# Weight splits, one softmax sum and the block means of v moved between engines in a fused attention and feed-forward kernel

## Chip, cores and metric

The kernel runs on one core of one Trainium2 chip. The metric is the device time of one execution in microseconds; a profile of one execution gives the times of single instructions. TensorE, VectorE, ScalarE and GpSimd are the engines that compute, SyncE (SP) issues the transfers. In the rows they are PE (PEld its weight loads), DVE, ACT, POOL and SP; a q behind a name is the engine's queue.

## The reference

```
k_sum = k in blocks of 32 tokens, max over the block     # 24 rows per head
v_sum = v in blocks of 32 tokens, mean over the block
scores = q k^T / 8, kept where |i - j| < 16; q k_sum^T / 8 + log 32
a = softmax over both kinds of scores together
x = a [v; v_sum]                       # 2 batches, 8 heads, 768 tokens, 64 wide
x = relu(x w_in)^2 w_out               # 1536 tokens, 512 -> 2048 -> 512
xn = x / rms(x) * rms_g
out = (silu(xn w_gate) * (xn w_val)) w_out2    # 512 -> 1536 -> 512
```

Inputs and output are float32, the weights float64 in memory: each is read as pairs of 32-bit words.

## The kernel before, in words

**Weights.** A unit is a weight tile of 128 x 512 (wi, wo of the first feed-forward; wg, wv, wp of the second), in the order of the list `order`. The class `Units` takes each through four steps: load the raw words (`load64`, L157), two ScalarE instructions (`conv_a`, L176 and L177), four VectorE instructions that put a float32 together (`conv_b`, L183 to L190), and `split` (L193): ScalarE casts to the format of the fast products (hi, L196), VectorE subtracts to get the rest (lo, L197). Every product is done as hi hi + hi lo + lo hi. Raw words, split weights and the raw q, k and v chunks share 14 buffers of tag "w".

**Attention** works on 12 groups of 128 tokens, 6 per batch. For a group g: `scores` (L417, TensorE), `softmax` (VectorE adds the mask L440 and takes the maximum; then either ScalarE does eight exponentials with the maximum as bias and sums by itself, L446, or VectorE subtracts L451, ScalarE does one exponential L452 and VectorE sums L453; `EXPACT(g)` says which; VectorE normalises, L454 to L456), `ptrans` (transposes L466, copy L467), `av` (products with the v rows in vx, L487, then split into xhi on ScalarE, L477, and xlo on VectorE, L478). Groups 0 to 2 do the softmax in two halves. `vload(g)` loads the group's v rows into vx, which holds two groups. Once per batch, the keys are loaded (`prep_load`), transposed (L327), reduced to block maxima (L330) and laid out with the maxima in gaps (L339, L340, `prep_kend` L344); the v means come from `vmean`: v is loaded in three chunks (`vm_load`) into "w" buffers, six products with an indicator matrix (L375) add rows of a block, and the result is copied to vm and from there to vx (L383, L384, `vmput` L390).

**Order.** Batch 1's first groups stand alone (L597 to L636). Then a loop over k_ from 0 to 5 (L695) interleaves a pair of groups each with the products of the first four wi (`h_pair`) and wo (`y_pair`) on the 256 tokens that are ready. Batch 2's keys are loaded at k_ 0, prepared within `y_pair(0, 2)`, its means formed at k_ 1 in front of group 7. After the loop come the other units of the first feed-forward (L759) and the second one (L790), on 512 tokens at a time.

The code is traced in this order, and a planner (L852) then orders each engine's instructions with its own cost model and puts in the waits: an instruction that it thinks ready can be placed ahead of earlier ones that wait. `issue_after` adds an edge on one engine's order. On the chip each engine's order is fixed, and the transfers of SP are one queue.

Of the kernel before, what the change touches and what calls it, by code (L numbers as in the profile page):

```python
# [32 lines left out]
def tile_window_attention_moe_moe2(  # L33
# [13 lines left out]
    nc = tc.nc  # L47
# [42 lines left out]
    um = cpool.tile([P, KW + QT], F32, name="um")  # L90
    masks = {}
    ind = cpool.tile([P, NB + P // (BLK // 2) * (NC2 - 1)], F32, name="ind")
    ss = cpool.tile([P, NG], F32, name="ss")
    rinv = cpool.tile([P, NG], F32, name="rinv")

    def constants():
        n = ind.shape[1]
        o = P // (BLK // 2) * (NC2 - 1)
        pb = BLK // 2
        nc.gpsimd.memset(ind, 1.0 / BLK)  # L100
        nc.gpsimd.affine_select(
            out=ind, in_=ind, compare_op=ALU.is_ge, fill=0.0, base=pb * o,
            pattern=[[-pb, n]], channel_multiplier=1,
        )
        nc.gpsimd.affine_select(
            out=ind, in_=ind, compare_op=ALU.is_ge, fill=0.0, base=pb - 1 - pb * o,
            pattern=[[pb, n]], channel_multiplier=-1,
        )
        nc.gpsimd.memset(um, 0.0)
        nc.gpsimd.affine_select(  # L110
            out=um, in_=um, compare_op=ALU.is_ge, fill=NEG, base=-1,
            pattern=[[1, KW + QT]], channel_multiplier=-1,
        )
        nc.gpsimd.affine_select(
            out=um, in_=um, compare_op=ALU.is_ge, fill=NEG, base=2 * WIN - 1,
            pattern=[[-1, KW + QT]], channel_multiplier=1,
        )


        mid = cpool.tile([P, NK], F32, name="mask_mid")  # L120
        nc.gpsimd.memset(mid, math.log(BLK))
        for j, n, o in ((0, G0, 0), (K1, QT, G0)):
            nc.gpsimd.tensor_copy(mid[0:QT, j : j + n], um[0:QT, o : o + n])
            nc.gpsimd.tensor_copy(mid[QT:P, j : j + n], um[QT:P, QT + o : QT + o + n])
        first = cpool.tile([P, NK], F32, name="mask_first")
        nc.gpsimd.tensor_copy(first, mid)
        nc.gpsimd.memset(first[0:QT, 0:WIN], NEG)
        last = cpool.tile([P, NK], F32, name="mask_last")
        nc.gpsimd.tensor_copy(last, mid)
        nc.gpsimd.memset(last[QT:P, NK - WIN : NK], NEG)  # L130
        masks.update(first=first, mid=mid, last=last)
# [58 lines left out]
        nc.vector.tensor_tensor(xi, xi, r, op=ALU.add)  # L190
        return x

    def split(x, nm):  # L193
        w_ = wslot(f"w_{nm}")
        hi, lo = w_[:, 0], w_[:, 1]
        nc.scalar.copy(hi, x)  # L196
        nc.vector.tensor_tensor(lo, x, hi.bitcast(F32), op=ALU.subtract)  # L197
        return hi, lo

    class Units:  # L200
# [9 lines left out]
        def tick(self):  # L210
            n, units = self.n, self.units
            if n[3] < n[2]:
                u = units[n[3]]
                W[u] = split(self.x.pop(u), "%s%d" % u)
                n[3] += 1
            if n[2] < n[1]:
                u = units[n[2]]
                self.x[u] = conv_b(*self.a.pop(u))
                n[2] += 1
            if n[1] < n[0]:  # L220
                u = units[n[1]]
                self.a[u] = conv_a(self.raw.pop(u), "%s%d" % u)
                n[1] += 1
            self.load(min(n[2] + self.ahead, len(units), self.used + self.cap))
# [9 lines left out]
                self.tick()  # L234

    def EXPACT(g):
        return g % 4 != 1

    def PARTS(g):
        return 2 if g < 3 else 1  # L240
# [101 lines left out]
    def prep_kend(b, eng, w0, w1):  # L342
# [3 lines left out]
            state[b].unsqueeze(2).to_broadcast([P, NPAIR, w1 - w0, NB]),  # L346
        )

    def vm_load(b, c):
        state[("v", b, c)] = raw_chunk(v, b, c, f"vr{b}_{c}")  # L350

# [14 lines left out]
    def vmean(b, c):  # L366

        if c == 0:
            state["vmps"] = psA(f"vmean{b}", [K1, DM])
        ps = state["vmps"][G0:K1]  # L370
        pb = BLK // 2
        nb2 = P // pb
        vr = state.pop(("v", b, c))
        for e in range(2):
            nc.tensor.matmul(  # L375
                ps, ind[:, nb2 * (NC2 - 1 - c) : nb2 * (NC2 - 1 - c) + NB], vr[:, :, e, :],
                start=(c == 0 and e == 0), stop=(c == NC2 - 1 and e == 1),
            )
        if c == NC2 - 1:
            vm = ap_.tile([K1, DM], F32, tag="vm", name=f"vm{b}", bufs=1)[G0:K1]  # L380
            state["vm"] = vm
            if b == 0:
                nc.vector.tensor_copy(vrows(0, 2), ps.unsqueeze(1).to_broadcast([NB, 2, DM]))  # L383
            nc.scalar.copy(vm, ps)  # L384

    def vrows(i0, n):
# [38 lines left out]
    def softmax(g):  # L425
        r = g % GPB
        mk = masks["first" if r == 0 else ("last" if r == GPB - 1 else "mid")]
        sl = state.pop(("s", g))
        te = ap_.tile([P, 2, NPAIR, NK], F32, tag="t", name=f"t{g}", bufs=TB)
        t = te.rearrange("q e p n -> q (e p) n")  # L430
        state[("t", g)] = t
        mx = ap_.tile([P, H], F32, tag="mx", name=f"mx{g}", bufs=TB)
        sm = ap_.tile([P, H], F32, tag="sm", name=f"sm{g}", bufs=TB)
        parts = PARTS(g)
        n = H // parts
        for i in range(parts):
            hs = slice(n * i, n * i + n)
            tv, m_, s_ = t[:, hs], mx[:, hs], sm[:, hs]
            for e in range(2 // parts * i, 2 // parts * (i + 1)):
                nc.vector.tensor_tensor(  # L440
                    te[:, e], sl[e], mk.unsqueeze(1).to_broadcast([P, NPAIR, NK]), op=ALU.add
                )
            if EXPACT(g):
                nc.vector.reduce_max(m_, tv, axis=AX.X, negate=True)  # L444
                for h in range(hs.start, hs.stop):
                    mark[("exp", g)] = nc.scalar.activation(  # L446
                        t[:, h], t[:, h], AF.Exp, bias=mx[:, h : h + 1], accum_out=sm[:, h : h + 1]
                    )
            else:
                nc.vector.reduce_max(m_, tv, axis=AX.X)  # L450
                nc.vector.tensor_tensor(tv, tv, m_.unsqueeze(2).to_broadcast([P, n, NK]), op=ALU.subtract)  # L451
                mark[("exp", g)] = nc.scalar.activation(tv, tv, AF.Exp)  # L452
                nc.vector.reduce_sum(s_, tv, axis=AX.X)  # L453
            nc.vector.tensor_scalar_add(s_, s_, 1e-9)  # L454
            nc.vector.reciprocal(s_, s_)
            mark[("norm", g)] = nc.vector.tensor_tensor(  # L456
                tv, tv, s_.unsqueeze(2).to_broadcast([P, n, NK]), op=ALU.mult
            )
# [235 lines left out]

    for k_ in range(NK2):  # L695
        g, last = 2 * k_ + 3, 2 * k_ + 3 >= NG
        if k_ == 0:
            for c in range(NC2):
                prep_load(1, c)
        h_pair(k_, 0)  # L700
        if k_ == 0:
            av(2)
            group(4)
        if not last:
            ptrans(g)
        if g == GPB - 1:
            group(GPB)
        h_pair(k_, 2)
        if not last:
            av(g)  # L710
        if g == GPB - 1:
            for c in range(NC2):
                vmean(1, c)
            vmput(0, 2)
        if g + 2 < NG:
            group(g + 2)
            if g + 2 == GPB + 1:
                vmput(2, 2)
        y_pair(k_, 0)
        if g + 1 < NG:  # L720
            ptrans(g + 1)
        if k_ == 0:
            prep_begin(1)
            prep_k(1, 0)
            y_pair(k_, 2, (lambda: prep_k(1, 1), lambda: prep_k(1, 2)))
            prep_kend(1, nc.gpsimd, 0, NW1)
            for c in range(NC2):
                vm_load(1, c)
        else:
            if g + 3 < NG:  # L730
                qprep(g + 3)
            y_pair(k_, 2)
        if g + 1 < NG:
            av(g + 1)
        if k_ == 0:
            qprep(GPB)
        elif g + 3 < NG:
            group(g + 3)
        if k_ == 2:
            units1.cap = NW - 3  # L740
        for _ in range(TICKS[k_]):
            units1.tick()
        if not last and g == NG - 1:
            actx.close()
            rot["tags"] = ("a",)
            side["pool"] = ctx.enter_context(
                tc.tile_pool(name="w2pool", bufs=1, side="right", reuse_waits="tile")
            )
            side["psum"] = ctx.enter_context(
                tc.tile_pool(name="psY2", bufs=1, space=PSUM, reuse_waits="tile")  # L750
            )
            grow = side["pool"].tile([P, DM], F32, tag="grow", name="grow")
            nc.sync.dma_start(grow, rms_g.partition_broadcast(P))
            units1.cap = NW + NRIGHT - 3
# [102 lines left out]
```

## Time and profile before

| | us |
|---|---|
| median of 3 runs | 668.42 (667.29 to 668.84) |
| the profiled execution | 668.78 |
| its span, first to last instruction | 667.1 |
| mean granted clock of TensorE | 0.982 of full speed |

The span is what the rows below lie in, in microseconds from its start; the 1.7 us around it belong to the execution. Busy time of an engine is summed over its instructions; records of TensorE are pipelined, so a full busy share there is not full speed by itself. Idle time counts only on the engine that the others wait for.

### The profile page before, as it was taken

How to read it: one execution, taken by the hardware profiler on the slowest of the kernel's cores; microseconds unless marked ns; L12 is line 12 of the kernel's file. 1: busy time of each engine (PE TensorE's matmuls, PEld its weight loads, DVE VectorE, ACT ScalarE, POOL GpSimd, SP SyncE). 2: the span in 40 equal slices, each digit the busy share in tenths (PEclk: the TensorE clock that was granted, in tenths of full speed). 3: DMA queues.
4: the chain of work that ended last, by engine and by line, in shares of the span. 5: the costliest groups of instructions: out<-in, count | busy, mean ns of one | idle time of the engine just before them, and what ended most of it. 6: DMA issues, size and time to landing. Idle time of an engine off the chain costs nothing.

```text
span 667.1 us, 9349 instructions
## 1 busy us (share of the span) xinstructions
PE 647.4 (97%) x3644; PEld 535.2 (80%) x3644; DVE 402.6 (60%) x729; ACT 306.5 (46%) x649; POOL 10.2 (2%) x29
## 2 busy tenths in 40 slices
PE   7789989999999999999999999999999999999997
PEld 6378857888888888888888888888888888888885
DVE  3999667759999279627574894289613171313132
ACT  4687667557775257226353873167411231111110
POOL 3000010000000000000000000000000000000000
PEclk8969999999999999999999999999999999999999
DMA  9993554315414123101120252015300000001011
GB/s 235 280 233 91 135 160 151 81 38 190 131 52 139 59 63 96 31 1 64 31 96 31 89 165 63 1 48 160 108 1 1 0 1 0 1 1 63 1 63 64
DMA packets 76956, 53.69 MB, mean 80 GB/s; under 512 B 45040, under 2 KB 71664, under 8 KB 76912
## 3 DMA queue, kind: packets, MB, share of 16 engines
q1 hardware_dynamic: 76912, 53.09, 26.9%
q8 instruction: 29, 0.48, 0.3%
q14 instruction: 15, 0.12, 0.1%
HBM read 49.94 MB, written 3.15 MB: 80 GB/s over the span
## 4 chain that ended last, share of the span: by engine, by line
PE 90%; DVE 4%; ACT 2%; DMA 1%; SPq 1%; issue 1%; DVEq 0%; ACTq 0%
PE y L529 19%; PE h L508 19%; PE v L508 15%; PE g L508 15%; PE z L529 14%; PE s L417 2%; PE vmean L375 2%; PE xps L487 2%; PE pps L466 1%; ACT t L446 1%; SPq L304 1%; DMA qr<-in_q_dram 1%; PE xps L499 1%; DVE mx L444 1%; DVE t L440 1%
## 5 line engine op out<-in xcount | busy, mean ns | idle before, releaser
L508 PE MATMUL h<-xhi,w_wi 128*128 128x512 f32 (+1 forms) x480 | 133.9, 352 | 0.0
L529 PE MATMUL y<-w_wo,hhi 128*128 128x512 f32 x384 | 118.0, 392 | 0.6 <-ACT hhi L519 0.6
L803 DVE TENSOR_TENSOR sg<-v,sg 128x512 f32<-128x512 f32 x36 | 24.9, 691 | 131.1 <-PE v L508 131.1
L508 PEld LDWEIGHTS h<-xhi,w_wi 128*128 128x128 f32 x480 | 86.2, 192 | 12.1 <-issue 0.3
L508 PE MATMUL v<-xhi,w_wv 128*128 128x512 f32 x288 | 94.7, 390 | 0.0
L508 PE MATMUL g<-xhi,w_wg 128*128 128x512 f32 x288 | 94.5, 390 | 0.0
L529 PE MATMUL z<-w_wp,hhiz 128*128 128x512 f32 x288 | 88.1, 389 | 0.0
L508 PE MATMUL h<-xlo,w_wi 128*128 128x512 f32 (+1 forms) x240 | 84.2, 352 | 2.8 <-DVE xlo L478 2.8
L529 PEld LDWEIGHTS y<-w_wo,hhi 128*128 128x128 f32 x384 | 71.2, 188 | 15.1 <-ACT hhi L519 0.9
L529 PE MATMUL y<-w_wo,hlo 128*128 128x512 f32 x192 | 73.4, 392 | 0.0
L801 ACT ACTIVATE sg<-g 128x512 f32<-128x512 f32 x36 | 21.5, 598 | 101.9 <-PE g L508 99.7
L508 PEld LDWEIGHTS v<-xhi,w_wv 128*128 128x128 f32 x288 | 54.1, 188 | 11.2
L529 PEld LDWEIGHTS z<-w_wp,hhiz 128*128 128x128 f32 x288 | 54.0, 188 | 11.2
L508 PEld LDWEIGHTS g<-xhi,w_wg 128*128 128x128 f32 x288 | 54.0, 188 | 11.1
L656 ACT ACTIVATE r<-h 128x512 f32<-128x512 f32 x48 | 28.7, 598 | 69.8 <-PE h L508 69.8
L508 PE MATMUL v<-xlo,w_wv 128*128 128x512 f32 x144 | 56.1, 389 | 0.0
L508 PE MATMUL g<-xlo,w_wg 128*128 128x512 f32 x144 | 56.0, 389 | 0.0
L529 PE MATMUL z<-w_wp,hloz 128*128 128x512 f32 x144 | 55.4, 389 | 0.0
L519 ACT CAST hhiz<-sg 128x512 fp32r<-128x512 f32 x36 | 22.3, 621 | 68.4 <-DVE sg L803 68.1
L657 DVE TENSOR_TENSOR r<-h,r 128x512 f32<-128x512 f32 x48 | 33.0, 687 | 34.1 <-ACT r L656 34.0
L508 PEld LDWEIGHTS h<-xlo,w_wi 128*128 128x128 f32 x240 | 46.1, 192 | 8.8 <-DVE xlo L478 3.0
L529 PEld LDWEIGHTS y<-w_wo,hlo 128*128 128x128 f32 x192 | 35.7, 188 | 7.3 <-issue 0.2
(129 smaller groups left out, 913.6 us busy)
## 6 DMA issues: line engine op xcount, KB each, us to landing
raw_wi<-in_moe_w_in_dram SPq DMA_DIRECT2D x16, 512.0 KB, 5.3
raw_wo<-in_moe_w_out_dram SPq DMA_DIRECT2D x16, 512.0 KB, 5.1
raw_wg<-in_moe_w_gate_dram SPq DMA_DIRECT2D x12, 512.0 KB, 3.6
raw_wv<-in_moe_w_val_dram SPq DMA_DIRECT2D x12, 512.0 KB, 3.5
raw_wp<-in_moe_w_out_dram SPq DMA_DIRECT2D x12, 512.0 KB, 3.5
kr<-in_k_dram SPq DMA_DIRECT2D x12, 256.0 KB, 4.2
qr<-in_q_dram SPq DMA_DIRECT2D x12, 256.0 KB, 4.1
vr<-in_v_dram SPq DMA_DIRECT2D x6, 512.0 KB, 5.9
```

What stands on the lines that cost most here:

```text
L304: nc.sync.dma_start(t[:, j].rearrange("p (h d) -> p h d", h=H), src[b, :, o : o + P, :].rearrange("h p d -> p h d"),)
L375: nc.tensor.matmul(ps, ind[:, nb2 * (NC2 - 1 - c) : nb2 * (NC2 - 1 - c) + NB], vr[:, :, e, :], start=(c == 0 and e == 0), stop=(c == NC2 - ...
L417: mark[("s", g)] = nc.tensor.matmul(sl[e][QT * u : QT * u + QT, p, :], qT[rr, p, QT * u : QT * u + QT], kT[rr, p, o : o + NK], start=True, ...
L440: nc.vector.tensor_tensor(te[:, e], sl[e], mk.unsqueeze(1).to_broadcast([P, NPAIR, NK]), op=ALU.add)
L487: nc.tensor.matmul(ps[QT * e : QT * e + QT, o : o + QT], vx[:, (2 * g + u) % NVX, 2 * p + e, :], pT[:, e * NPAIR + p, QT * u : QT * u + QT ...
L508: nc.tensor.matmul(ps, a_, b_, start=(i == 0), stop=(i == tot - 1))
L519: nc.scalar.copy(hi[:, 0:n], s[:, 0:n])
L529: nc.tensor.matmul(y, a_[:, ms], b_, start=(first and i == 0), stop=(last and i == 2))
L656: nc.scalar.activation(t, ps, AF.Relu)
L657: nc.vector.tensor_tensor(t, ps, t, op=ALU.mult)
L801: nc.scalar.activation(t, psg, AF.Silu)
L803: nc.vector.tensor_tensor(t, psv, t, op=ALU.mult)
```

## The change

- The first eight units (four wi, four wo) are split on GpSimd, copy and subtraction. The last GpSimd subtraction is kept as the mark "split".
- The first unit's `conv_b` is ordered on VectorE behind the last maximum of group 0.
- Group 1's softmax takes the ScalarE form (eight exponentials with sums).
- Batch 1's copy of the means into vx goes from VectorE (L383) to ScalarE.
- Batch 2's keys are loaded after group 5 instead of at the head of the loop.
- Batch 2's v is loaded by two transfers after group 4 into two x buffers (tags xhi and xlo), as 96 partitions of 8 tokens each, four heads to a buffer. GpSimd adds the 8 tokens in three steps (4, 2, 1 left) for each buffer, ordered behind "split"; two products of 256 columns with a new indicator over 96 partitions give the means, in place of six of 512 columns.

```diff
+    NE = 8
+    PV = S // NE
+    indv = cpool.tile([PV, NB], F32, name="indv")
...
+        pv = BLK // NE
+        nc.gpsimd.memset(indv, 1.0 / BLK)
+        nc.gpsimd.affine_select(out=indv, in_=indv, compare_op=ALU.is_ge, fill=0.0, base=0,
+            pattern=[[-pv, NB]], channel_multiplier=1)
+        nc.gpsimd.affine_select(out=indv, in_=indv, compare_op=ALU.is_ge, fill=0.0, base=pv - 1,
+            pattern=[[pv, NB]], channel_multiplier=-1)
...
-    def split(x, nm):
+    def split(x, nm, pool):
         w_ = wslot(f"w_{nm}")
         hi, lo = w_[:, 0], w_[:, 1]
-        nc.scalar.copy(hi, x)
-        nc.vector.tensor_tensor(lo, x, hi.bitcast(F32), op=ALU.subtract)
+        if pool:
+            nc.gpsimd.tensor_copy(hi, x)
+        else:
+            nc.scalar.copy(hi, x)
+        low = (nc.gpsimd if pool else nc.vector).tensor_tensor(lo, x, hi.bitcast(F32), op=ALU.subtract)
+        if pool:
+            mark["split"] = low
         return hi, lo
...
-                W[u] = split(self.x.pop(u), "%s%d" % u)
+                W[u] = split(self.x.pop(u), "%s%d" % u, n[3] < 2 * ROUNDS1[0])
...
-                self.x[u] = conv_b(*self.a.pop(u))
+                with after(*((("mx", 0),) if n[2] == 0 else ())):
+                    self.x[u] = conv_b(*self.a.pop(u))
...
     def EXPACT(g):
-        return g % 4 != 1
+        return g % 4 != 1 or g == 1
...
+    HH = H // 2
+    vsum = [xpool.tile([P, KD, CH], F32R, tag=t, name=f"vsum{t}") for t in ("xhi", "xlo")]
+    vsum = [
+        t.bitcast(F32).rearrange("p k s -> p (k s)").rearrange("p (h e d) -> p h e d", h=HH, e=NE)[0:PV]
+        for t in vsum
+    ]
+
+    def vs_load(b):
+        for i, t in enumerate(vsum):
+            nc.sync.dma_start(
+                t.rearrange("p h e d -> p h (e d)"),
+                v[b, HH * i : HH * (i + 1)].rearrange("h (p e) d -> p h (e d)", e=NE),
+            )
+
+    def vs_add():
+        for t in vsum:
+            n = NE
+            while n > 1:
+                n //= 2
+                nc.gpsimd.tensor_tensor(t[:, :, 0:n], t[:, :, 0:n], t[:, :, n : 2 * n], op=ALU.add)
+
+    def vs_mean(b):
+        ps = psA(f"vmean{b}", [K1, DM])[G0:K1]
+        for i, t in enumerate(vsum):
+            nc.tensor.matmul(
+                ps[:, HH * D * i : HH * D * (i + 1)], indv, t[:, :, 0, :], start=True, stop=True
+            )
+        vm = ap_.tile([K1, DM], F32, tag="vm", name=f"vm{b}", bufs=1)[G0:K1]
+        state["vm"] = vm
+        nc.scalar.copy(vm, ps)
...
-                nc.vector.tensor_copy(vrows(0, 2), ps.unsqueeze(1).to_broadcast([NB, 2, DM]))
+                nc.scalar.copy(vrows(0, 2), ps.unsqueeze(1).to_broadcast([NB, 2, DM]))
...
-                nc.vector.reduce_max(m_, tv, axis=AX.X, negate=True)
+                mark[("mx", g)] = nc.vector.reduce_max(m_, tv, axis=AX.X, negate=True)
...
-        if k_ == 0:
-            for c in range(NC2):
-                prep_load(1, c)
         h_pair(k_, 0)
         if k_ == 0:
             av(2)
             group(4)
+            vs_load(1)
...
         if g == GPB - 1:
-            for c in range(NC2):
-                vmean(1, c)
+            vs_mean(1)
             vmput(0, 2)
         if g + 2 < NG:
             group(g + 2)
+            if k_ == 0:
+                for c in range(NC2):
+                    prep_load(1, c)
...
             prep_kend(1, nc.gpsimd, 0, NW1)
-            for c in range(NC2):
-                vm_load(1, c)
+            with after("split"):
+                vs_add()
```

## Rows read from the trace of the kernel before

**Rows 1.** The page's chain that ended last: shares of the span by engine.

```profile
PE 90%; DVE 4%; ACT 2%; DMA 1%; SPq 1%; issue 1%; DVEq 0%; ACTq 0%
```

**Rows 2.** Table by stage: window, its length, busy us by engine (instructions), clock, DMA.

```profile
24.50:46.70 22.20, 17.38 (x167) 14.23 (x167) 22.14 (x50) 18.89 (x50) 1.51 (x1) 0.69 1.01 290
46.70:72.00 25.30, 25.30 (x270) 22.84 (x271) 24.85 (x44) 18.07 (x49) 0.00 (x0) 1.00 0.42 103
72.00:93.50 21.50, 21.50 (x203) 14.85 (x202) 10.69 (x17) 13.43 (x40) 1.28 (x2) 1.00 0.64 160
93.50:101.00 7.50, 4.74 (x27) 4.53 (x26) 6.54 (x12) 5.57 (x21) 2.35 (x2) 0.77 0.37 137
158.00:667.00 509.00, 504.88 (x2263) 418.52 (x2261) 285.52 (x518) 203.63 (x360) 0.00 (x0) 1.00 0.18 58
```

**Rows 3.** Chain of waits, 0 to 160 us: start, length, what.

```profile
45.93 0.70 DVE xlo L478
...
47.33 4.18 PE h L508 x35
```

**Rows 4.** VectorE's subtractions of line L197, 14 to 72 us: ns min/median/max, starts.

```profile
L197 DVE TENSOR_TENSOR w_wi<-x_wi,w_wi x4: 680/681/684, 25.1 to 43.6; 128x512 fp32r<-128x512 f32 x4
L197 DVE TENSOR_TENSOR w_wo<-x_wo,w_wo x4: 645/667/686, 50.7 to 65.3; 128x512 fp32r<-128x512 f32 x4
```

**Rows 5.** VectorE's groups by form, 14 to 72 us: busy us, mean ns, idle before.

```profile
L451 DVE TENSOR_TENSOR t<-t,mx 128x480 f32<-128x480 f32 x2 | 1.4, 746 | 0.0
...
L453 DVE TENSOR_REDUCE sm<-t 128x4 f32<-128x480 f32 x2 | 1.3, 630 | 0.0
L383 DVE COPY vx<-vmean 24x1024 f32<-24x1024 f32 x1 | 1.2, 1217 | 0.1
```

**Rows 6.** ScalarE's groups by form, 14 to 47 us.

```profile
L446 ACT ACTIVATE t<-t,mx 128x120 f32<-128x120 f32 x21 | 8.0, 386 | 4.3 <-DVE mx L444 4.3
...
L196 ACT CAST w_wi<-x_wi 128x512 fp32r<-128x512 f32 x4 | 2.5, 613 | 0.0
...
L452 ACT ACTIVATE t<-t 128x480 f32<-128x480 f32 x2 | 1.2, 604 | 0.7 <-DVE t L451 0.7
```

**Rows 7.** Timeline of GpSimd and VectorE, 25.1 to 26.9 us: start, length.

```profile
25.20 1.51 POOL L390 COPY vx<-vm 24x1024 f32<-24x1024 f32 x1 [13.13 <-ACT vm L384]
...
26.38 0.84 DVE L451 TENSOR_TENSOR t<-t,mx 128x480 f32<-128x480 f32 x1
```

**Rows 8.** Lines L390 and L190 by themselves: ns min/median/max, starts.

```profile
L390 POOL COPY vx<-vm x3: 1035/1492/1513, 25.2 to 94.4; 24x1024 f32<-24x1024 f32 x3
...
L190 DVE CUSTOM_DVE_ANT_0 x_wi<-x_wi,u_wi x9: 678/683/785, 16.9 to 160.6; 128x1024 uint16<-128x1024 uint16 x9
```

**Rows 9.** GpSimd's groups by form, whole span.

```profile
L344 POOL COPY kT<-ksum 128x768 f32<-128x768 f32 x1 | 0.9, 939 | 6.0 <-DVE ksum L330 6.0
...
L126 POOL COPY mask_first<-mask_mid 128x120 f32<-128x120 f32 x1 | 0.3, 284 | 0.1
```

**Rows 10.** Chain of waits, 84 to 104 us.

```profile
87.32 5.26 PE vmean L375 x12
...
96.74 4.87 PE h L508 x26
```

**Rows 11.** TensorE's waits, 90 to 101 us: in total, times, longest.

```profile
PE h L508 <- DVE xlo L478: 2.8, 1, 2.8
```

**Rows 12.** Timeline of SP's transfers, 0 to 200 us: start, time to issue, count.

```profile
0.81 5.30 SPq L304 DMA_DIRECT2D kr<-in_k_dram  x6
...
31.74 9.57 SPq L304 DMA_DIRECT2D kr<-in_k_dram  x6
...
45.65 17.11 SPq L403 DMA_DIRECT2D vx<-in_v_dram  x12
```

**Rows 13.** The tile kr: time from issue to landing of its transfers.

```profile
DMA to landing us min/median/max: 3.1/4.2/7.3
```

**Rows 14.** Chain of waits, 0 to 160 us, batch 2's last key transposes.

```profile
76.35 0.87 PE kps L327 x8
```

More of the change, by code (lines that the diff above doesn't have):

```diff
@@ L107, in constants @@
             pattern=[[pb, n]], channel_multiplier=-1,
+        )
+        pv = BLK // NE
+        nc.gpsimd.memset(indv, 1.0 / BLK)
+        nc.gpsimd.affine_select(
+            out=indv, in_=indv, compare_op=ALU.is_ge, fill=0.0, base=0,
+            pattern=[[-pv, NB]], channel_multiplier=1,
+        )
+        nc.gpsimd.affine_select(
+            out=indv, in_=indv, compare_op=ALU.is_ge, fill=0.0, base=pv - 1,
+            pattern=[[pv, NB]], channel_multiplier=-1,
         )
@@ L347, in prep_kend @@
         )
+    HH = H // 2
[9 more added lines that the diff above has]
+                v[b, HH * i : HH * (i + 1)].rearrange("h (p e) d -> p h (e d)", e=NE),
+            )
+    def vs_add():
[9 more added lines that the diff above has]
+                ps[:, HH * D * i : HH * D * (i + 1)], indv, t[:, :, 0, :], start=True, stop=True
+            )
+        vm = ap_.tile([K1, DM], F32, tag="vm", name=f"vm{b}", bufs=1)[G0:K1]
+        state["vm"] = vm
+        nc.scalar.copy(vm, ps)
     def vm_load(b, c):
```

## The prediction

> **What bounds the kernel now.** I read the chain's shares first. TensorE carries 90% of the chain that ended last [rows 1], so an edit counts only where TensorE waits, runs at a low granted clock, or loses work. The table by stage says where: from 158 us on it is busy 504.9 of 509 us at clock 1.00 [rows 2], and the diff touches nothing there. What can move is the first 158 us.
>
> There the bound changes hands. From 24.5 to 46.7 us VectorE is busy 22.1 of 22.2 us while TensorE runs at a mean clock of 0.69 with gaps; from 46.7 to 72 VectorE is still at 24.9 of 25.3, but TensorE is now solid; from 72 to 93.5 TensorE is solid alone and VectorE has half its time free [rows 2]. The chain hands over when VectorE writes the low half of group 1's attention result at 45.93, after which the first feed-forward products run without a break [rows 3]. So the first stage is VectorE's, and a microsecond taken from its work before 72 us should reach the end nearly whole. The last soft place is 93.5 to 101: TensorE idles 2.8 us for VectorE's xlo and then runs at half clock (mean of the stage 0.77; the two levels are 2.4 and 1.2 GHz) [rows 2, 11].
>
> **Part 1, VectorE's work before 72 us.** Removed: eight subtractions L197, 4 x 0.681 + 4 x 0.667 = 5.4 us [rows 4]; for group 1 the two L451 (1.4) and two L453 (1.3), because the exponentials on ScalarE subtract and sum by themselves, 2.7 us in all (L450 becomes L444, the same reduction); the copy L383, 1.2 us [rows 5]. Together 9.3 us.
>
> What takes it over: ScalarE loses eight casts at 0.613 (4.9 us), gains eight exponentials for group 1 (8 x 0.386 = 3.1) less two L452 (1.2), and gains the copy of 24x1024. That copy has no ScalarE row; L452's 0.604 for 480 elements puts it between 0.6 and 1.3, I take 1.1 [rows 6]. Net 1.9 us less, on an engine busy 18.9 of 22.2 us [rows 2]: no new bound.
>
> GpSimd gets eight copies and eight subtractions of 128x512. A copy costs 0.28 us at 120 elements and 0.94 at 768, so 0.68 at 512 on the line between [rows 9]. No GpSimd instruction with two inputs is in this trace: its lower end is that copy, 0.68, its upper end two copies, 1.36; I take the middle, 1.0, since it must read twice but starts once. A split is then 1.7 us, eight are 13.4 us, spread over some 40 us on an engine otherwise idle. As a queue that is short: a split now waits on VectorE behind other work, and GpSimd has nothing ahead of it.
>
> The Trainium skill, GPSIMD Engine Reference (section 3.1), gives some 2.6 cycles per element for two inputs; an estimate from it is 1.1 us for the subtraction, 14.3 us for the eight splits, and the sum below would then be some 0.3 us longer.
>
> **The price of that** is in the trace. The copy L390 takes 1.035 us once and 1.49 to 1.51 twice; one of the slow ones is that at 25.20. The other way round, VectorE's L451 at 26.38 starts while this copy runs and takes 0.84, where the mean of the two L451 is 0.746, so the other took 0.65; and one L190 of nine takes 0.785 instead of 0.683 [rows 5, 7, 8]. So GpSimd loses some 0.46 us in a collision and VectorE 0.10 to 0.19, where the L451 had met only the last 0.33 us of the copy. With sixteen GpSimd instructions the bounds are 0 (none collides) and 16.3 us (each stops VectorE for its whole length at the upper price). I take 0.3 us each, 4.8 us: more than the two rows show, since a conversion is four VectorE instructions on SBUF data in a row and will often meet more than a tail. Part 1 is 9.3 - 4.8 = 4.5 us faster.
>
> The Trainium skill speaks against this change here: SBUF — State Buffer, "Who interferes with whom", says that a VectorE instruction with two SBUF inputs, or in a two-port mode, and a GpSimd instruction that reads SBUF lock each other out, the second waiting for the whole of the first. The rows agree in kind. By this rule alone the time would be that of the first rival.
>
> The order edge (conversion of the first weight behind group 0's second maximum) lets group 0 start earlier by at most a conversion, 4 x 0.683 = 2.7 us at L190's duration [rows 8], and puts that work later by as much. Between 2.7 faster and 2.7 slower I take 0, because VectorE does the same work before 72 us. The three more GpSimd instructions for the new indicator run before anything needs them: 0.
>
> **Part 2, the means of batch 2.** Twelve records of 512 columns, 5.26 us of solid TensorE time, go [rows 10]. Two products of 256 columns are four records at half of 0.44, 0.9 us. That is 4.4 us off a stretch where TensorE has no slack. Behind it, the scores of group 7 now come 4.4 us earlier, and on VectorE's queue the mask add, the maximum and then xlo wait for them. If VectorE's order stays, the idle 2.8 us and the slow 26 products after it simply move: they took 4.87 us, and 35 such products took 4.18 at full clock, so 26 would take 3.1 and 1.8 us is lost to the clock [rows 3, 10, 11]. The planner sees a shorter vmean and may put xlo ahead; also the three 512 KB buffers that batch 2's v held are free for raw weights, for one of which ScalarE waits in this stretch. So 0 to 4.6 us more; I take half, 2.3. Part 2 is 6.7 us faster.
>
> The adds for it: two tiles, each 1024, 512 and 256 elements, 3584 in all. At the copy's rate (0.66 us per 648 elements) 3.6 us, at twice that 7.3; I take 5.5. They stand behind the last split, which I expect near 61 us (65.3 - 4.5), and are wanted near 83, so they cost nothing. If the planner puts them behind the gap copy L344 instead, which cannot run before the last transposes (76.35 - 4.5 and some 2 us), they end near 79.5, still in time; that cover is 3.3 us (87.3 - 4.5 = 82.8). Queued behind them is only that copy, which the scores of group 6 need.
>
> **Part 3, transfers.** v for batch 2 is the same 1.57 MB in two transfers without a wait on the weight buffers. The six key transfers leave the saturated stretch (DMA share 1.01 [rows 2]); SP issued them from 31.74 on. Moved behind group 5's v rows, they start after 45.65 + 17.11 = 62.8 us of the old time, take 5.3 us to issue (as the first six did) and 4.2 to land: the last by 72.3, against the last transposes at 76.35 [rows 12 to 14]. Cover 4.1 us, cost 0; without it up to 6 us (third rival). The planner already issues transfers ahead of waiting ones, so the keys may move less than the code says, which costs nothing either.
>
> **Sum.** 4.5 + 6.7 = 11.2 us off the profiled execution's own 668.78: 657.6. The median of the runs is 668.42, 0.36 lower, so this is 10.8 us, 1.6%, below it. A difference under 0.2% (1.3 us) is what a measurement of this kernel cannot tell from none.
>
> **Rivals.**
> 1. *GpSimd holds VectorE* (slower). Place: 24.5 to 72 us. If each of the sixteen split instructions stops VectorE for its whole length at the upper price, 8 x (0.68 + 1.36) = 16.3 us, part 1 becomes 16.3 - 9.3 = 7.0 slower, part 2 keeps its 4.4: 671.4. It decides from a loss of 13.7 us, 0.86 per GpSimd instruction. For it: VectorE is 99% busy there. Against: the two collisions seen cost it 0.10 and 0.19. Chance 0.16; a further 0.08 for losses near that point, which give no difference.
> 2. *The first stage gains nothing.* The locks take 9.3 us, or ScalarE, 85% busy there, takes over as the bound; and the stall at 94 stays. Only 4.4 remains: 664.4. For it: VectorE's lost time is bounded only widely. Chance 0.17.
> 3. *The keys are late.* If their buffers come free only after the last split, now at 65.3 [rows 4], and they land as slowly as the slowest did (7.3 [rows 13]), the last is there at 77.9, against 76.35 - 4.5 = 71.9: TensorE waits 6.0 us: 663.6. Chance 0.08.
> 4. *All of it.* Locks cost nothing and the stall with its slow clock goes: 9.3 + 9.0 = 18.3, 650.5. For it: the free buffers and the earlier start of group 0. Against: TensorE must then find its inputs ready throughout. Chance 0.14.
>
> **The numbers.** The forecast's own case (653 to 661.5) has 0.37. Faster by over 0.2%: 0.37 + 0.17 + 0.08 + 0.14 = 0.76; within it 0.08; slower 0.16. A range of 648 to 668 takes in the forecast, rivals 2 to 4 and below them most of the order edge, and leaves out about 0.2.
>
> **What would show it.** Right: no L197 or L196 on VectorE and ScalarE before 70 us, the unbroken first products starting 4 us or more earlier, vmean at 0.9 us, some L187, L190 or L456 stretched by 0.1 to 0.6 us beside GpSimd instructions. Wrong: those stretched by over 0.86 us per GpSimd instruction (rival 1), the products starting at 46 us or later (2), TensorE waiting at the key transposes for DMA (3), or a stall before vmean that GpSimd's adds end.

## The result, and the profile after

The changed kernel is slower: 673.19 us, median of 4 runs (673.06 to 675.70), against 668.08 (667.29 to 668.84) before it. The ratio is 1.0075, 95% interval 1.0055 to 1.0094. The forecast was 657.6, and the time lies above the upper end of its range, 668. The profiled execution took 673.06 us, its span is 671.4 and TensorE's mean granted clock 0.991 (before 0.982).

The table by stage answers [rows 2] (window, length, busy us of TensorE, its weight loads, VectorE, ScalarE, GpSimd, clock, DMA):

```profile
24.50:46.70 22.20, 15.35 (x184) 13.20 (x185) 19.76 (x38) 19.32 (x67) 8.39 (x8) 0.85 1.00 274
46.70:72.00 25.30, 21.04 (x222) 16.99 (x221) 23.56 (x31) 13.51 (x35) 18.51 (x14) 0.93 0.92 187
72.00:93.50 21.50, 20.60 (x232) 17.36 (x231) 21.47 (x37) 17.70 (x44) 5.18 (x4) 1.00 0.59 163
93.50:101.00 7.50, 7.36 (x63) 6.99 (x61) 6.49 (x13) 6.96 (x28) 0.00 (x0) 1.00 0.42 129
158.00:667.00 509.00, 509.00 (x2232) 414.56 (x2230) 282.32 (x512) 201.19 (x356) 0.00 (x0) 1.00 0.17 56
```

The stall at 94 to 101 is gone, as forecast: 7.36 of 7.5 us busy at full clock. In exchange TensorE is no longer solid from 46.7 to 72 (21.04 against 25.30), and VectorE, which had half its time free from 72 to 93.5, is now full there. The last row is the one that matters. From 158 us on, TensorE is busy all of 509 us (the idle end of this longer span lies behind the window), and yet it gets through fewer products (2232) than before in 504.88 us (2263).

The chain of waits around the means, which answers [rows 3, 10, 14]:

```profile
41.16 0.60 DVE xlo L528
...
88.53 0.97 PE vmean L392 x4
89.50 0.89 PE y L579 x3
90.39 1.43 PE s L467 x30
91.83 1.36 PE y L579 x5
93.18 5.76 PE h L558 x48
```

Group 1's low half comes 4.8 us earlier (41.16, before 45.93). Nothing of that is left where the means begin (88.53, before 87.32); but they take 0.97 us instead of 5.26, and the unbroken products behind them start at 93.18 instead of 96.74. Counted back from the end, the 2200th product starts 165.03 us into the span, before it was 169.38: **up to there the change is 4.4 us ahead.** Those last 2200 products then take 501.62 us, before 493.11: **8.5 us are lost where the diff touches no instruction.** The two chains of waits show how. Here is that of the kernel before, in the first feed-forward:

```profile
181.32 2.72 PE y L529 x12
184.04 2.72 PE h L508 x12
186.76 2.72 PE y L529 x12
189.49 2.72 PE h L508 x12
```

and that of the changed kernel:

```profile
180.04 2.80 PE h L558 x12
182.83 2.79 PE y L579 x12
185.63 2.81 PE h L558 x12
188.44 2.81 PE y L579 x12
191.25 2.72 PE h L558 x12
```

Twelve products of 128x512 take 2.80 us instead of 2.72, at the same granted clock (1.00) and with no wait between them; a few pieces still take 2.72.

GpSimd's and VectorE's timelines show the price of the moved work. The first block holds GpSimd's subtractions (L213) and adds (L387), the second VectorE:

```profile
40.84 1.27 POOL L213 TENSOR_TENSOR w_wi<-x_wi,w_wi 128x512 fp32r<-128x512 f32 x1
...
48.27 2.08 POOL L213 TENSOR_TENSOR w_wo<-x_wo,w_wo 128x512 fp32r<-128x512 f32 x1
...
62.61 2.83 POOL L387 TENSOR_TENSOR vsumxhi<-vsumxhi 96x1024 f32<-96x1024 f32 x1
65.41 2.38 POOL L387 TENSOR_TENSOR vsumxlo<-vsumxlo 96x1024 f32<-96x1024 f32 x1
...
71.83 0.73 POOL L387 TENSOR_TENSOR vsumxlo<-vsumxlo 96x256 f32<-96x256 f32 x1
```

```profile
49.12 1.50 DVE L197 TENSOR_SCALAR x_wo<-x_wo 128x512 uint32<-128x512 uint32 x1
...
52.09 0.41 DVE L197 TENSOR_SCALAR x_wo<-x_wo 128x512 uint32<-128x512 uint32 x1
...
65.75 3.05 DVE L506 TENSOR_TENSOR t<-t,sm 128x960 f32<-128x960 f32 x1
...
78.57 1.15 DVE L506 TENSOR_TENSOR t<-t,sm 128x960 f32<-128x960 f32 x1
```

L197 takes 1.50 us beside a subtraction of GpSimd and 0.41 with GpSimd idle. The normalisation L506 takes 3.05 beside the add of 2.38, and 1.15 where it began before GpSimd did (at 78.57; with GpSimd idle it takes as long). GpSimd's subtraction takes 1.27 at its shortest and 2.08 in the collision. Added up over the VectorE instructions that overlap GpSimd's, each against the median of its form beside an idle GpSimd, the sixteen split instructions cost VectorE 7.3 us and the six adds 2.3.

### The profile page after: what moved, and what is told of

Same layout as the page of the kernel before. It is cut to its first block, busy times and chain, and to the rows that moved or that the text cites. A ratio compares the mean times of both kernels' runs of the same rounds, so it can differ in the third digit from the quotient of the medians.

```text
span 671.4 us, 9342 instructions
## 1 busy us (share of the span) xinstructions
PE 645.4 (96%) x3636; PEld 527.6 (79%) x3636; DVE 405.2 (60%) x716; ACT 305.1 (45%) x656; POOL 38.1 (6%) x54
## 4 chain that ended last, share of the span: by engine, by line
PE 83%; DVE 8%; SPq 3%; ACT 3%; issue 1%; DMA 1%; DVEq 0%; ACTq 0%
PE y L579 18%; PE h L558 18%; PE v L558 15%; PE g L558 15%; PE z L579 15%; ACT t L496 1%; SPq L323 1%; SPq L453 1%; DVE t L490 1%; DVE t L506 1%; PE xps L537 1%; DMA raw_wi<-in_moe_w_in_dram 1%; DVE mx L494 1%; PE xps L549 1%; PE pps L516 1%
## 5 line engine op out<-in xcount | busy, mean ns | idle before, releaser
L579 PE MATMUL y<-w_wo,hhi 128*128 128x512 f32 x384 | 121.0, 399 | 1.3 <-ACT hhi L569 1.3
L579 PE MATMUL y<-w_wo,hlo 128*128 128x512 f32 x192 | 75.2, 400 | 0.5 <-DVE hlo L570 0.5
L851 ACT ACTIVATE sg<-g 128x512 f32<-128x512 f32 x36 | 21.5, 598 | 104.8 <-PE g L558 102.6
```

The source lines that it names most:

```text
L579: nc.tensor.matmul(y, a_[:, ms], b_, start=(first and i == 0), stop=(last and i == 2))
L851: nc.scalar.activation(t, psg, AF.Silu)
```

## Experiments: the products after 158 us

Each run is timed beside the kernel before on one chip, and its ratio is against that; the runs are on several chips, and a difference between two of them is one of medians (the kernel before had 668.08 beside the change, 668.68 to 669.02 in the experiments). Two theories: (a) the price lies in the moved work of the first 158 us; (b) the new constant indv, 96 bytes per partition, moves buffers, and the products of the whole kernel feel it. In the built programs' allocation the small constants before the change end at byte 20480; behind them lie, on the left, 14 weight buffers and the activations (xhi, xlo, hhi, hlo). Nine more weight buffers, used once attention is done, are placed from the right, the first at byte 192000. The two operands of the late products of 128x512 lie a multiple of 512 bytes apart, whatever their sides. With indv everything behind it on the left lies 96 bytes higher and the right stays.

**Run 1, the changed kernel with indv elsewhere.** It takes 24 of the 120 floats of an unused strip at the right edge, so that no other buffer moves against the kernel before; each engine's order is that of the changed kernel.

```diff
-    lpool.tile([P, 120], F32, name="edge")
+    lpool.tile([P, 96], F32, name="edge")
-    indv = cpool.tile([PV, NB], F32, name="indv")
+    indv = lpool.tile([PV, NB], F32, name="indv")
```

> The changed kernel with the new indicator in the place of a part of the unused edge tile, so that every other buffer lies where it lay before the change; instructions and their order are those of the changed kernel. Theory A (layout): the 96 bytes of the indicator shift all weight and x buffers of the left side, and a 128x512 product whose moving and stationary operands lie at different remainders of 64 bytes takes 233 ns and not 227. Then all products are back at 227 ns, the 8.6 us lost after 148 us are gone and the time is 663 to 665 us. Rival B (the slow products come from something else, such as TensorE's activity or the chip): 672 to 674 us with products of 227 to 238 ns as before.

663.50 us against 669.02, ratio 0.992 [0.9899, 0.994]: faster than before, and 9.7 us faster than the changed kernel (10.6 if each is taken against the kernel before on its own chip). Its chain is back at the old pace:

```profile
174.94 2.72 PE y L579 x12
177.66 2.72 PE h L558 x12
180.38 2.72 PE y L579 x12
```

**Run 2, the kernel before with 96 unused bytes** among its constants and nothing else:

```diff
-    ss = cpool.tile([P, NG], F32, name="ss")
+    cpool.tile([P, 24], F32, name="gap"); ss = cpool.tile([P, NG], F32, name="ss")
```

> The kernel before with an unused tile of 96 bytes in front of the small constants, nothing else. Theory A (layout): weight and x buffers of the left side move by 96 bytes, the right side does not; products of mixed sides take 233 ns, the time is 675 to 679 us. Rival B: 667 to 669 us, all products at 227 ns.

679.50 us, ratio 1.015 [1.0126, 1.0173]. An unused tile costs 10.5 us, and its chain has the pieces of the changed kernel:

```profile
184.94 2.81 PE y L529 x12
187.75 2.80 PE h L508 x12
190.55 2.79 PE y L529 x12
```

Theory (b) holds. What about the shift is it that counts: the buffers' own position, or that of the two sides against each other? Three runs of the changed kernel move the right side down as well, by a longer strip at the edge, in the same order of instructions.

**Run 3, right side 32 bytes down.**

```diff
-    lpool.tile([P, 120], F32, name="edge")
+    lpool.tile([P, 128], F32, name="edge")
```

> The changed kernel with the edge tile of the right side 32 bytes longer, so that the buffers of both sides lie at remainder 32 of 64 bytes. Theory A in its form 'only the difference between the two operands counts': products at 227 ns, 663 to 666 us. Theory A2, 'an operand off a 64-byte boundary is slow by itself': products at 233 ns or more throughout, 675 us or more. Rival B: 672 to 674 us.

674.27 us, 1.0077 [1.0058, 1.0095]: no gain. Equal remainders of 64 bytes are not enough; the time is near the one expected of rival B, but runs 1 and 2 speak against that rival.

**Runs 4 and 5, right side 416 and 160 bytes down** (the same line with 224 and with 160 floats).

> The changed kernel with the right side moved down by 416 bytes, so that left buffers lie 96 bytes and right buffers 32 bytes past a 64-byte boundary's grid of 2048 in such a way that the difference between any two operands of a product is a multiple of 512 bytes, as it was before the change. Theory A3 (the difference between the two operands, modulo 512, sets the pace; the boundary itself does not): all products at 227 ns, 662 to 666 us. Theory A2 (being off the boundary counts, in any pair across the sides): products across the sides at 233 ns, 672 us or more.

> As the run with the right side moved by 416 bytes, but by 160, so that operands of different sides differ by a multiple of 256 that is none of 512. If a multiple of 256 is enough: products at 227 ns and 662 to 666 us; if 512 is needed: products across the sides slower, 668 to 675 us.

666.72 us, 0.9963 [0.995, 0.9976], and 664.72, 0.9938 [0.9915, 0.9962] (two runs). The first lies just above the expected range, the second within it. Both have 2.72 in the chain again; this is the chain with the strip of 160 floats:

```profile
181.86 2.72 PE y L579 x12
184.58 2.72 PE h L558 x12
187.30 2.72 PE y L579 x12
```

The starts of the last 1989 products, matched with the addresses of their two operands, tell the kernels apart (mean ns to the next product; "same": both operands on the left, 964 products; "across": one left, one right, 1025; then the last 2200 together):

```
kernel          left up  right down  distance moved   same    across   last 2200
before           0 B       0 B          0 B          226.8    226.8    493.11 us
indv at edge     0         0            0            226.8    226.8    493.11
changed         96         0           96            227.7    233.5    501.62
before + gap    96         0           96            227.7    233.5    501.62
right 32        96        32          128            227.5    232.8    500.67
right 160       96       160          256            226.8    226.8    493.09
right 416       96       416          512            226.8    226.8    493.09
```

The products that take one operand from either side are slowed by 6 to 7 ns, the others by under 1 ns. With both sides off their old position, but 256 or 512 bytes further apart, nothing is lost; with 128 the loss is nearly that of 96. All seven rows fit one rule: in this kernel the distance between the two operands, taken modulo 256 bytes, decides. Five distances stand behind it. That the sides matter in themselves can't be the reason, since the same products across them take 226.8 in four rows.

## Experiments: what the parts are worth

From here on indv lies at the edge or is not there, so that the late stage is that of the kernel before (493.11 us for the last 2200 products in each of these runs); "run 1" (663.50) is the whole change.

**Seven of the eight splits back on ScalarE and VectorE** (the eighth stays, as the mark behind which the adds are ordered).

```diff
-                W[u] = split(self.x.pop(u), "%s%d" % u, n[3] < 2 * ROUNDS1[0])
+                W[u] = split(self.x.pop(u), "%s%d" % u, n[3] == 2 * ROUNDS1[0] - 1)
```

> The aligned changed kernel with seven of the eight splits back on ScalarE and VectorE; only the last stays on GpSimd, so that the adds keep their place behind it. Theory C (GpSimd's splits lock VectorE for about as long as they save it): within 2 us of the aligned changed kernel. Rival D (the locks of the splits cost more than the 4.7 us that they save): 3 us or more faster than it. Rival E (the splits are the gain): 3 us or more slower, up to 4.7.

661.72, 0.9892 [0.9871, 0.9913]: 1.8 us faster than run 1. The intervals overlap, so the splits on GpSimd gain nothing, and may cost something. TensorE is busy 24.60 us from 46.7 to 72 instead of run 1's 20.85.

**The adds left out.**

```diff
-            with after("split"):
-                vs_add()
```

> The aligned changed kernel without GpSimd's six adds: the means of batch 2 are then formed from one token of eight, so the adds are left out of the computation. Theory F (the adds hold VectorE's two-input instructions from 60 to 70 us, as the normalisation that took 3.03 us and not 1.15 shows): 2 to 4 us faster than the aligned changed kernel. Theory of the prediction (the adds cost nothing): within 1 us of it.

661.12, 0.9881 [0.9862, 0.99]: in their place behind the last split the adds cost some 2.4 us by medians (the interval just touches run 1's), where the forecast had 0. In the profiled executions the means start at 82.8 us without the adds and at 86.4 with them (run 1).

**Group 1's softmax as before.**

```diff
-        return g % 4 != 1 or g == 1
+        return g % 4 != 1
```

> The aligned changed kernel with group 1's softmax in its old form. By the prediction it frees 2.7 us of VectorE before 47 us: 2 to 3 us slower than the aligned changed kernel. If ScalarE's three extra microseconds stand on the path instead: the same or faster.

665.92, 0.9958 [0.9941, 0.9974]: the sums of group 1 on ScalarE are worth 2.4 us; the forecast had 2.7.

**Only the edits without GpSimd**: the kernel before with group 1 on ScalarE, batch 1's copy of the means on ScalarE, the order edge and the later keys; and the same with the keys at the loop's head, as before.

```diff
-        return g % 4 != 1
+        return g % 4 != 1 or g == 1
...
-                nc.vector.tensor_copy(vrows(0, 2), ps.unsqueeze(1).to_broadcast([NB, 2, DM]))
+                nc.scalar.copy(vrows(0, 2), ps.unsqueeze(1).to_broadcast([NB, 2, DM]))
...
-                self.x[u] = conv_b(*self.a.pop(u))
+                with after(*((("mx", 0),) if n[2] == 0 else ())):
+                    self.x[u] = conv_b(*self.a.pop(u))
```

> The kernel before with group 1's sums on ScalarE, the copy of batch 1's means on ScalarE, the order edge and the later keys; splits on ScalarE and VectorE, means by six products, no new buffer. VectorE is freed of 2.7 + 1.2 us and meets no lock. Theory G (that relief reaches the end): 3 to 5 us faster than before. Theory H (the rest of the change is what gains, this alone does not): within 1.3 us of before.

The second of the two, against the first:

```diff
+        if k_ == 0:
+            for c in range(NC2):
+                prep_load(1, c)
         h_pair(k_, 0)
...
-            if k_ == 0:
-                for c in range(NC2):
-                    prep_load(1, c)
```

> As the run without GpSimd work, but with the keys of batch 2 loaded at the head of the loop as before. If the later keys gain or cost nothing (the prediction's part 3): within 1.3 us of that run. If they leave room for the transfers that the first groups wait for: slower than that run by more.

666.64, 0.9964 [0.9948, 0.998], and 666.47, 0.9975 [0.9956, 0.9994]. A gain of some 2 us, between the two expectations of the first run, and the place of the keys changes nothing that can be measured.

**The new means alone**, in the kernel before (vs_load, vs_add and vs_mean as in the change, with no edge on the adds):

```diff
-            for c in range(NC2):
-                vmean(1, c)
+            vs_mean(1)
...
-            for c in range(NC2):
-                vm_load(1, c)
+            vs_add()
```

> The kernel before with the new means of batch 2 alone (v in x buffers, adds on GpSimd, two products; the indicator in the edge's place; splits, group 1, keys and the order edge as before). The prediction's part 2: 6.7 us faster than before, 4.4 at least. Theory F (the adds' locks and the later stall give part of it back): 2 to 5 us faster.

678.65, 1.0142 [1.0123, 1.0162]: 9.9 us slower, where both expectations had it faster, though TensorE has 4.3 us less to do at full clock. Without the splits the adds are no longer held back. They run at 50 to 62 us, across the stage that VectorE fills:

```profile
50.46 5.91 POOL L381 TENSOR_TENSOR vsumxhi<-vsumxhi 96x1024 f32<-96x1024 f32 x3 [24.95 <-DMA vsumxhi<-in_v_dram]
56.33 5.41 POOL L381 TENSOR_TENSOR vsumxlo<-vsumxlo 96x1024 f32<-96x1024 f32 x3
```

```profile
50.76 3.33 DVE L500 TENSOR_TENSOR t<-t,sm 128x960 f32<-128x960 f32 x1
54.01 1.76 DVE L203 CUSTOM_DVE_ANT_0 x_wo<-x_wo,u_wo 128x1024 uint16<-128x1024 uint16 x1
...
56.90 2.59 DVE L196 TENSOR_SCALAR x_wo<-x_wo 128x512 f32<-128x512 f32 x1
...
60.01 1.15 DVE L210 TENSOR_TENSOR w_wo<-x_wo,w_wo 128x512 fp32r<-128x512 f32 x1
```

Against 1.15, 0.68, 0.41 and 0.67 undisturbed, these four lose 5.9 us (2.18, 1.08, 2.18 and 0.48).

**The same with the adds behind batch 2's gap copy** (an edge on that copy, kend), **and without them** (the line vs_add() left out).

```diff
-            vs_add()
+            with after("kend"):
+                vs_add()
```

> The kernel before with the new means of batch 2 alone, as in the run that was 10 us slower, but the adds ordered on GpSimd behind the gap copy of batch 2, where VectorE has half its time free. Theory F (that run's loss came from the adds' locks at 50 to 62 us): 3 to 7 us faster than before, unless the means then wait for the adds. If v's new place or its transfers cause the loss: still 675 us or more.

> The same with the adds left out (the means of batch 2 are formed from one token of eight; the adds are left out of the computation). Theory F: 4 us or more faster than before, and 13 us or more faster than with the adds at 50 to 62 us. If the planner's order without the old means causes the loss: 675 us or more.

674.75, 1.0081 [1.0062, 1.0099], and 671.74, 1.0024 [1.0, 1.0047]. Both expectations missed. The adds' early place costs 3.9 us and the adds altogether 6.9, near the 5.9 read from VectorE; but even without them the new means gain nothing in the old kernel. The trace without adds shows what is late next. This is its chain of waits:

```profile
76.19 4.10 DMA raw_wi<-in_moe_w_in_dram
80.31 0.67 ACT x_wi L189
...
85.28 0.47 ACT xhi L521
85.75 0.51 ACT qT L407
86.39 1.04 PE s L461 x16
87.43 1.00 PE pps L510 x4
88.43 1.80 PE s L461 x16
```

SP loads three raw weights from 73.55 on, into the three buffers that batch 2's keys had held. In the kernel before, batch 2's v took one of these buffers and two others, and the first raw weight was issued at 82.98. Their conversions now stand on ScalarE ahead of the copy of the transposed queries (qT), for which TensorE waits 2.3 us. Behind that wait sixteen score products take 1.80 us where the same took 1.04 at 86.39, and from 93.5 to 101 us the granted clock is 0.50 of full speed, the lower of the two levels. So the 4.3 us taken from TensorE come back as a wait and a slow stretch. No run held these three loads back, so this is read from the trace and not shown by an experiment. In run 1 the same loads start at 70.64 and TensorE runs through (21.27 of 21.5 us busy from 72 to 93.5).

**A version with half the adds and one split**: v as three chunks of 128 partitions with two tokens each, three adds of 512 elements, three products of 512 columns, and the seven splits back.

```diff
-                n //= 2
-                nc.gpsimd.tensor_tensor(t[:, :, 0:n], t[:, :, 0:n], t[:, :, n : 2 * n], op=ALU.add)
+            nc.gpsimd.tensor_tensor(t[:, :, 0], t[:, :, 0], t[:, :, 1], op=ALU.add)
...
+            nc.tensor.matmul(ps, ind[:, o : o + NB], t[:, :, 0, :], start=c == 0, stop=c == NC2 - 1)
```

> The aligned changed kernel with seven splits back and the adds cut to one step: v of batch 2 as three chunks of 128 partitions by two tokens in the x buffers, three adds of 512 elements, three products of 512 columns. The adds shrink from 7168 to 1536 elements (both buffers together), TensorE does 1.7 us more than with two products. Theory F (locks by adds cost some 2.4 us, as the run without them shows): 0 to 2 us faster than the run with seven splits back. If the adds' locks do not matter: 1 to 2 us slower than it.

(The elements added per partition were 3584 and become 1536; the expectation's 7168 is wrong.) 660.38 us, 0.9873 [0.9852, 0.9894]: the fastest kernel of the study, 8.3 us faster than the kernel before on the same chip (668.68) and 12.8 below the change. From the run with seven splits back (661.72) it can't be told apart.

## Why the prediction was wrong, point by point

**The step that failed** is in part 1: "The three more GpSimd instructions for the new indicator run before anything needs them: 0", together with, in the first paragraph, "from 158 us on [...] the diff touches nothing there". No run shows a cost of the instructions, but the tile they fill was not priced, and among the ways in which an edit can count (a wait, a low clock, work lost) the pace of the products themselves was left out. Its 96 bytes moved the activations against the nine weight buffers on the right, and each product that takes one operand from either side took 6.7 ns longer (233.5 for 226.8). Run 1 against the change puts this at 9.7 us, run 2 at 10.5; 8.5 us of it are in the last 2200 products. Added to the forecast, 9.7 gives 667.3, so this step makes most of the miss of 15.6 us; and the sign turns on it, since without it (run 1) the whole change is faster than the kernel before.

**What is left, some 5 us** (run 1 gains 5.5 of the 10.8 forecast), are terms of the sum:

- *The splits.* The forecast took 5.4 us off VectorE and gave 4.8 back for locks, a gain of 0.6. Measured: no gain, by the medians a cost of 1.8. GpSimd's copy took 0.61 us at its shortest (0.68 forecast) and its subtraction 1.27 (1.0), near the upper end of 1.36. The lock was underpriced at 0.3 us per instruction: one collision takes up to 1.1 us from a short VectorE instruction (L197, 1.50 for 0.41), and the sixteen together take 7.3 us, 0.45 each, which is more than the 5.4 removed. The Trainium skill, SBUF — State Buffer, "Who interferes with whom", says the second of the two waits for the whole of the first; the rows here agree, and the forecast's tails of 0.10 to 0.19 [rows 5, 7, 8] were too kind a sample.
- *The adds.* "So they cost nothing" was wrong: they cost 2.4 us. The cover was reckoned for the means, which did find them in time (72.56 against 88.53). But they held VectorE up for 2.3 us between 62 and 73 us, where TensorE waits for it. They also took 10.1 us, not 5.5.
- *Group 1* was sized right (2.4 for 2.7), so was *vmean* (0.97 for 0.9), and *the keys* cost nothing, as said.
- *The stall at 94* went, worth in its own stage 2.6 us of busy time (7.36 for 4.74; 2.3 forecast), but from 46.7 to 72 us TensorE lost 4.4 us of busy time (20.85 for 25.30 in run 1) to waits for VectorE: there the transposes of the softmax result (pps) wait 2.9 us for the normalisation and 1.6 for xlo. So the premise of part 1, that a microsecond taken from VectorE before 72 us reaches the end nearly whole, failed too: the 4.8 us gained at group 1's low half were gone at the means.

By medians 2.4 (splits) + 2.4 (adds) + 0.3 (group 1) = 5.1 of the 5.3 us that are missing. Each of these differences is near the width of an interval, so the agreement is no proof of each; for the splits (5.4 - 7.3 = -1.9) and the adds (2.3) VectorE's timeline says the same.

**The rivals.** Rival 1 (671.4) is the nearest in time and its mechanism is there, but it isn't the cause: it decides from 0.86 us per GpSimd instruction and the splits cost 0.45, without the layout's price the whole change is faster than before, and the change is ahead at 165 us, past the stage that the rival names. Rival 3 did not come. No rival named the addresses.

**Open.** In front of the last 2200 products the change is 2.0 us behind run 1, with the same order of instructions. Of these, 1.5 are there by the 61st product, 12 us into the span: the first keys land in 4.8 us (median), in run 1 in 3.8. The run with the right side 160 bytes down is 1.3 us behind at that product too (4.6 us), and its late products lose nothing. So these microseconds are not the price of slow products; whether they belong to the layout or to the single execution is not shown. The kernel with the right side 416 bytes down is 2.0 us slower than that with 160 at equal product times and equal order; its first stage runs at a lower clock (0.71 against 0.85 from 24.5 to 46.7), and why was not tried.

## What to carry to other kernels

A new tile is also a change of address for everything allocated behind it: before a small constant is called free, look where the buffers of the hot loop (the products that run longest) go, and put it where nothing moves. When a stage that the diff does not touch changes its pace at an unchanged clock, measure the kernel before with an unused tile of the same size. And work given to GpSimd while VectorE is the bound has to be priced as VectorE's time, collision by collision, and not as the time of an idle engine.

## What had not been expected of the hardware

A product of 128x512 takes 226.8 ns when its two operands lie in this kernel's old distance, a multiple of 512 bytes, or 256 or 512 bytes off it, and 233.5 ns (232.8) when they lie 96 (128) bytes off it. Neither operand's own position mattered: all left buffers 96 bytes higher with the right 160 lower run at 226.8. How it goes for other distances, or for other shapes, no run here shows.
